# Another order of the first loads, dummy matmuls, and a last row-pass step of 128 queries in an attention and mixture-of-experts kernel

## The chip, the core and the metric

The kernel runs on one core of a Trainium2 chip. The core has a matrix engine (PE, or TensorE), a vector engine (DVE), a scalar engine (ACT) and a general engine (POOL). The profile books the weight loads of PE apart, as PEld. Transfers between the memory of the chip and the core are issued by queues, most of them by the SP queue, and run on 16 DMA engines. The metric is the device time of one execution in microseconds, as the median of several executions.

## What is computed

Three layers follow one another, all in 32-bit floats. The reference, cut to what matters:

```python
# attention: 4 batches, 8 heads, 576 positions, head size 64, causal by blocks of 64
scores = scale * np.matmul(q, k.transpose(0, 1, 3, 2))
scores = np.where(block_i >= block_j, scores, -1000000000.0)
attn = np.exp(scores - np.max(scores, axis=-1, keepdims=True))
attn = attn / (np.sum(attn, axis=-1, keepdims=True) + 1e-09)
x = np.matmul(attn, v)                       # -> rows of 512, 2304 of them
# first mixture: 8 experts (512 -> 1024 -> 512), the two best of noisy logits
logits = x @ w_gate
noisy_logits = logits + np.log1p(np.exp(x @ w_noise)) * noise
out[mask] += top2_w[mask, k, None] * (np.maximum(x[mask] @ w1[e], 0.0) @ w2[e])
# second mixture: 8 experts, the best one, with a bias for each modality
logits = x @ w_gate + modality_bias[modality_id]
out[mask] = gate_w[mask, None] * (np.maximum(x[mask] @ w1[e], 0.0) @ w2[e])
```

## The kernel before

The attention takes the first 280 us or so, the two mixtures the rest. In the attention two heads are worked on together, as a **pair**: 4 batches with 4 pairs each are 16 pairs, numbered p from 0. To keep the accuracy of 32 bits, most operands are split into a high part, rounded to the type fp32r, and a low part, the rest; a product is then three matmuls (high by high, high by low, low by high).

The function `pair` (from line 877) holds the steps of a pair, each with a short name:

- **TQ, TK, T4** on PE transpose the queries, the keys, and the last 64 positions of both (the tiles qld, kld and tld). **QH, KH, A4** on ACT copy the high parts out, **QL, KL, D4** on DVE compute the low parts. The queries go to tiles that the trace calls kp, the keys to kh and kl.
- **S0 to S8** on PE compute the scores of blocks of queries (tile ps; S0 and S2 hold two blocks each, S8 takes two banks). **M** on DVE finds the row maximum (nm), **E** on ACT computes the exponentials (p) and their sums.
- **B0 to B5 and BT** on PE transpose the exponentials, **H** on ACT and **L** on DVE split them (PTh, PTl).
- **VX, V0, V1** on PE multiply by the values (tile pa), **CX, C0, C1** on ACT copy the result out (oT).
- **X0, X1** on PE are the **row pass** (function `xr`, line 1074), one for each head: they turn the 576 columns of oT back into rows and multiply by the gate weights at once, with IW (80 columns) as the moving operand. The stationary operand is a piece of oT: four pieces of 128 queries, and a last one of the 64 queries that remain. **XC0, XC1** on ACT copy the rows out (xu). Each of these matmuls of plain 32-bit floats stands as two instructions in the trace, so that one row pass is ten.

Three PSUM banks serve the scores, three the transposes and the row pass, one the values. A step that needs a bank waits until the one that last used it has been read.

The order of PE, ACT and DVE is written out by a **planner** while the program is built. It keeps a clock for each engine (`clk`), charges each instruction a cost (`pe_cost`, `act_cost`, `dve_cost`, from line 74), and of the steps whose inputs are done takes the one that can start first; among those that can start within 0.15 us it takes the one that is due first by the table SCHED (line 19). For the first pairs it takes the arrival of the loads from a constant, `arrive` (line 1267) plus 5.5 us for each pair; `earliest` (line 1301) uses it, `emit` (line 1279) writes the step. An engine works in that order alone: if one step waits, all that stand behind it on that engine wait. The queue SP is such a line too, and it issues all loads of queries, keys and values (`load`, line 849).

Ahead of the first step, nine dummy matmuls of 512 columns run on PE (line 1108), and the loads of the pairs 0 to 2 are issued in the order keys and queries of 0, values of 0, keys and queries of 1, values of 1, keys and queries of 2. Each load of queries, keys or values is two transfers of 128 KB, and the last 64 positions come in two transfers of 32 KB.

Of the kernel before, what the change touches and what calls it, by code (L numbers as in the profile page):

```python
# [7 lines left out]
F32 = mybir.dt.float32  # L8
# [22 lines left out]
def moe_kernel(tc, q, k, v, w_gate, w_noise, noise, w1, w2, mod_id, w_gate2, mod_bias, m2w1, m2w2, out):  # L31
# [42 lines left out]
    def cols_of(t):  # L74
        n = 1
        for x in t.shape[1:]:
            n *= x
        return n
# [7 lines left out]
    def pe_cost(name, o, i, kw):  # L86
        n = cols_of(o)
        dt = i.dtype
        if name == "transpose":
            return n * .00084  # L90
        return 2 * max(cols_of(i) * .00084, n * .00084) if dt == F32 else n * .000417 + .0145 * (clk["base"] is None)

    def act_cost(name, o, i, kw):
        tables = (not isinstance(kw.get("bias", 0.0), float)) + (not isinstance(kw.get("scale", 0.0), float)) + ("accum_out" in kw)
# [9 lines left out]
    with ExitStack() as top:  # L104
# [6 lines left out]
        LG = dram.tile([NT + CAP, E + 1], F32, name="LG")  # L111


        nc.scalar.preload_act_table_set("natural_log_exp_and_others")
        jp = cst.tile([128, 128], F32, name="jp")
        nc.gpsimd.iota(jp, pattern=[[1, 128]], base=0, channel_multiplier=-1, allow_small_or_imprecise_dtypes=True)
        ident = cst.tile([128, 128], F32, name="ident")
# [686 lines left out]
        with ExitStack() as ph:  # L804
# [41 lines left out]
            def copy(o, i):  # L846
                act.activation(o, i, AF.Copy)

            def load(p, names):
                b, hp = divmod(p, HP)  # L850
                r = L.setdefault(p, {})
                src = {"q": q, "k": k, "v": v}

                if names == "v":
                    r["v"] = ld.tile([128, 5, 2, D], F32, name="vld", bufs=2)
                    tails = [(r["v"][64 * i:64 * i + 64, 4], "v") for i in range(2)]
                else:
                    r["t"] = ld.tile([128, 2, D], F32, name="tld")
                    tails = [(r["t"][64 * i:64 * i + 64], n) for i, n in enumerate("qk")]
                    for n in names:  # L860
                        r[n] = ld.tile([128, 4, 2, D], F32, name=n + "ld")

                def ends():
                    for t, n in tails:
                        nc.sync.dma_start(t, src[n][b, 2 * hp:2 * hp + 2, 512:576, :].rearrange("h p d -> p h d"))
                if p:
                    ends()
                for n in names:
                    for i in range(2):
                        nc.sync.dma_start(r[n][:, 0:4, i, :],  # L870
                                          src[n][b, 2 * hp + i, 0:512, :].rearrange("(c p) d -> p c d", p=128))
                if not p:
                    ends()

            def pair(p):
# [198 lines left out]
                def xr(h):  # L1074
                    def X_():
                        pt = st["x", h] = ps_t.tile([128, 5, DG], F32, name="pt")
                        for c in range(5):
                            n = 128 if c < 4 else 64
                            ten.matmul(pt[0:n, c], st["oT"][:, h, 128 * c:128 * c + n], IW[:, 2 * hp + h], start=True, stop=True)

                    def C_():
                        pt = st["x", h]
                        copy(xu[:, h, 0:4], pt[:, 0:4])
                        copy(xu[0:64, h, 4], pt[0:64, 4])
                        st["xn"] = st.get("xn", 0) + 1
                        if st["xn"] == 2:
                            out_rows()
                    f["X%d" % h], f["XC%d" % h] = X_, C_
# [14 lines left out]


            nc.vector.memset(ones, 1.0)
            pw = ps_s.tile([128, 4, 128], F32, name="ps")
            for _ in range(9):
                nc.tensor.matmul(pw, ones, bc(ones[:, None, :], [128, 4, 128]), start=True, stop=True)
            load(0, "kq")
            load(0, "v")  # L1110
            load(1, "kq")
            load(1, "v")
            load(2, "kq")
            zeros(0, gps)
# [149 lines left out]
            nbank = {"s": bk[0], "t": bk[1], "a": bk[2]}  # L1264
            held = {"s": [], "t": [], "a": []}
            fin, steps = {}, {}
            arrive = dict(zip(("TK", "TQ", "T4"), (4.2, 5.7, 6.8)))
            todo = {e: [] for e in ("pe", "act", "dve")}
            for p in range(NPAIR):
                for n, o in OFF.items():  # L1270
# [8 lines left out]
            def emit(p, n, t):  # L1279
                if p not in steps:  # L1280
                    steps[p] = pair(p) if p < NPAIR else first_steps()
                clk["base"] = t
                steps[p][n]()
                fin[p, n] = clk[engine(n)]
                if n in E_ and all((p, x) in fin for x in E_):
                    emit(p, "R", t)
                if n in ("V0", "V1", "VX") and all((p, x) in fin for x in ("V0", "V1", "VX")) and p + 2 < NPAIR:
                    emit(p + 2, "VS", t)
                if n == "VS" and p + 2 < NPAIR:
                    load(p + 2, "v")  # L1290
                if n in ("TQ", "TK", "T4") and all((p, x) in fin for x in ("TQ", "TK", "T4")) and p < NPAIR:
                    if p + 3 < NPAIR:
                        load(p + 3, "kq")
                    elif p == NPAIR - 1:
                        fetch_b(3)
# [3 lines left out]
                return r[n] if isinstance(r, dict) else r + n[1:]  # L1299

            def earliest(e, p, n):
                t = clk[e] if p > 2 or n not in arrive else max(clk[e], arrive[n] + 5.5 * p)
                for d, k in before[n]:
                    if p >= k:
                        if (p - k, d) not in fin:
# [387 lines left out]
```

## Time and profile before

| | |
|---|---|
| median of three runs | 1004.54 us (1000.55 to 1005.47) |
| the profiled execution | 1002.42 us, its span 1000.6 us |
| PE busy | 955.4 us, 95% |
| DVE, ACT, POOL busy | 723.9, 518.6, 492.9 us |

The span is the time from the first to the last instruction; 1.8 us of the profiled execution lie around it. PE is the busiest engine by far, but a share of 95% hides stages that differ: the first 25 us, in which PE waits and at times runs at a lower granted clock; the pairs that follow, from 34 to 150 us; a stretch from 150 to 250 us in which DVE also routes rows to experts; and the mixtures. The columns of a window are its bounds, its length, the busy time of each engine with the number of instructions, the granted clock of TensorE (1.00 is 2.4 GHz, 0.50 is 1.2 GHz), the busy share of the DMA engines and GB/s. In the first 5 us the clock column reads 1.00 too, but the pace of the dummies says more there: nine of them take 3.89 us, 0.43 us each, and a matmul of 512 columns takes that long at 1.2 GHz.

### The profile page before, as it was taken

What the parts mean: (1) busy time and instruction counts of PE and PEld (TensorE: products, weight loads), DVE (VectorE), ACT (ScalarE), POOL (GpSimd) and SP (SyncE); (2) the same over time, 40 slices, a digit from 0 to 9 for tenths busy, and PEclk for the clock granted to TensorE, in tenths of its full rate; (3) what the DMA queues carried; (4) which work ended last, traced back from release to release, by engine and by line L of the source; (5) the groups of instructions that cost most, each with busy time, mean ns of one, the idle gap of its engine ahead of it and who ended that gap; (6) DMA issues with size and microseconds to landing.
All of it is one profiled execution on the core that took longest, in us unless ns stands there. A gap on an engine that the chain in (4) does not pass through costs nothing.

```text
span 1000.6 us, 17459 instructions
## 1 busy us (share of the span) xinstructions
PE 955.4 (95%) x6058; PEld 863.6 (86%) x6058; DVE 723.9 (72%) x1761; ACT 518.6 (52%) x1156; POOL 492.9 (49%) x400
## 2 busy tenths in 40 slices
PE   7999998898999999999999999999999989999995
PEld 5988898787888997989899898989979879999994
DVE  5878879999968985568493957759788876455450
ACT  5989887778653253333333343333325445555551
POOL 6133141432221589768594857747476254333321
PEclk8999999999999999999999999999999999999998
DMA  5557743331067556555472745534366867776620
GB/s 126 103 156 229 208 122 82 77 82 50 26 202 254 95 138 187 131 138 115 107 147 75 161 105 127 123 80 64 110 149 178 288 215 241 225 223 216 209 84 13
DMA packets 158257, 141.59 MB, mean 142 GB/s; under 512 B 76233, under 2 KB 124745, under 8 KB 158034
## 3 DMA queue, kind: packets, MB, share of 16 engines
q1 hardware_dynamic: 140098, 107.18, 36.4%
q0 software_dynamic: 18064, 33.23, 16.5%
q8 instruction: 50, 0.82, 0.3%
q14 instruction: 45, 0.37, 0.1%
HBM read 112.54 MB, written 28.36 MB: 141 GB/s over the span
## 4 chain that ended last, share of the span: by engine, by line
PE 72%; DVE 13%; issue 5%; ACT 3%; POOL 3%; DMA 2%; SPq 1%; POOLq 0%; ACTq 0%
PE ph L71 28%; PE py L71 26%; PE pt L71 7%; PE ps L71 5%; PE pa L71 3%; PE px L71 2%; DVE nm L71 2%; DVE PTl L71 2%; DVE wl L71 2%; POOL wl L71 2%; ACT p L71 1%; DVE kp L71 1%; DMA xr<-X,ids 1%; ACT wh L71 1%; POOL LG L71 1%
## 5 line engine op out<-in xcount | busy, mean ns | idle before, releaser
L71 POOL TENSOR_TENSOR wl<-raw,wh 128x1024 fp32r<-128x1024 f32 x80 | 207.8, 2628 | 107.7 <-ACT wh L71 93.5
L71 PE MATMUL ph<-xth,wh 128*128 128x320 f32 (+2 forms) x800 | 240.9, 301 | 2.1 <-DVE kp L71 2.1
L71 PE MATMUL ph<-xth,wl 128*128 128x320 f32 (+2 forms) x800 | 239.7, 300 | 0.0
L71 PE MATMUL ph<-xtl,wh 128*128 128x320 f32 (+2 forms) x800 | 239.7, 300 | 0.0
L71 DVE SCALAR_TENSOR_TENSOR zero<-py,gts,wide 128x512 f32<-128x512 f32 x304 | 227.4, 748 | 8.3
L71 PE MATMUL py<-wh,kp 128*128 128x512 f32 x496 | 166.8, 396 | 0.0
L71 PEld LDWEIGHTS ph<-xth,wh 128*128 128x128 f32 x800 | 151.6, 189 | 3.7 <-DVE kp L71 2.9
L71 ACT ACTIVATE wh<-raw 128x1024 fp32r<-128x1024 f32 x144 | 150.9, 1053 | 2.8 <-DMA raw<-in_moe_w_dram 2.8
L71 PEld LDWEIGHTS ph<-xtl,wh 128*128 128x128 f32 x800 | 151.6, 190 | 0.7
L71 PEld LDWEIGHTS ph<-xth,wl 128*128 128x128 f32 x800 | 151.6, 189 | 0.0
L71 ACT ACTIVATE yr<-py,gts 128x512 f32<-128x512 f32 x60 | 41.4, 690 | 144.9 <-PE py L71 96.8
L71 PEld LDWEIGHTS py<-wh,kp 128*128 128x128 f32 x496 | 93.2, 188 | 18.3
L71 DVE SCALAR_TENSOR_TENSOR hl<-ph,hh 128x320 fp32r<-128x320 f32 (+2 forms) x100 | 46.3, 465 | 79.2 <-ACT hh L71 79.0
L71 PE MATMUL ps<-kh,kp 128*128 128x256 f32 (+5 forms) x320 | 98.4, 349 | 3.5 <-ACT p L71 1.5
L71 DVE TENSOR_TENSOR wl<-raw,wh 128x1024 fp32r<-128x1024 f32 x64 | 79.7, 1253 | 29.6 <-ACT wh L71 29.5
L71 PE MATMUL py<-wl,kp 128*128 128x512 f32 x248 | 96.7, 390 | 0.0
L71 POOL DMA_INDIRECT xr<-X,ids x55 | 58.7, 1066 | 72.9 <-PE px L71 44.2
L71 PE MATMUL py<-wh,hh 128*128 128x512 f32 x232 | 93.9, 405 | 0.0
L71 PE MATMUL py<-wl,hh 128*128 128x512 f32 x232 | 90.5, 390 | 1.7 <-POOL wl L71 1.7
L71 PE MATMUL py<-wh,hl 128*128 128x512 f32 x232 | 90.7, 391 | 0.0
L71 ACT ACTIVATE hh<-ph 128x320 fp32r<-128x320 f32 (+2 forms) x100 | 41.9, 418 | 93.6 <-PE ph L71 90.4
L71 DVE TENSOR_TENSOR xtl<-px,xth 128x512 fp32r<-128x512 f32 x58 | 40.0, 689 | 68.1 <-ACT xth L71 68.0
(249 smaller groups left out, 1822.0 us busy)
## 6 DMA issues: line engine op xcount, KB each, us to landing
raw<-in_moe_w_dram SPq DMA_DIRECT2D x144, 512.0 KB, 4.0
X<-zero SPq DMA_DIRECT2D x13, 512.0 KB, 4.3
kld<-in_k_dram SPq DMA_DIRECT2D x32, 128.0 KB, 2.8
qld<-in_q_dram SPq DMA_DIRECT2D x32, 128.0 KB, 2.9
vld<-in_v_dram SPq DMA_DIRECT2D x32, 128.0 KB, 2.7
X<-x SPq DMA_DIRECT2D x16, 256.0 KB, 2.4
wide<-in_moe_w_dram SPq DMA_DIRECT2D x4, 512.0 KB, 4.7
wide<-WG2T POOLq DMA_DIRECT2D x1, 2048.0 KB, 11.6
```

The costliest lines, as they stand in the source:

```text
L71: return f(*a, **kw)
```

## The change

Four edits. The row pass takes as its last piece the last 128 queries of the 576 instead of the last 64 (the first half of them is computed a second time), and the copy behind it reads partitions 64 to 127. The planner's charge for a 32-bit matmul becomes 2 × max(0.09945, 0.00084 × columns). The queries of pair 0 are issued on ACT's queue ahead of ACT's table load, and on SP the keys and queries of pair 1 come ahead of the values of pair 0; the constants `arrive` are replaced by one for each of the pairs 0 to 2. Dummy matmuls: eight instead of nine at the start, in a bank of another pool, and a few more wherever the planner sees PE without work for over 0.6 us in the first 60 us of its clock.

```diff
-        return 2 * max(cols_of(i) * .00084, n * .00084) if dt == F32 else n * .000417 + .0145 * (clk["base"] is None)
+        return 2 * max(.09945, n * .00084) if dt == F32 else n * .000417 + .0145 * (clk["base"] is None)
...
-        nc.scalar.preload_act_table_set("natural_log_exp_and_others")
...
-            def load(p, names):
+            def load(p, names, eng=nc.sync):
...
-                        nc.sync.dma_start(r[n][:, 0:4, i, :],
+                        eng.dma_start(r[n][:, 0:4, i, :],
...
                         for c in range(5):
-                            n = 128 if c < 4 else 64
-                            ten.matmul(pt[0:n, c], st["oT"][:, h, 128 * c:128 * c + n], IW[:, 2 * hp + h], start=True, stop=True)
+                            c0 = 128 * c if c < 4 else S - 128
+                            ten.matmul(pt[:, c], st["oT"][:, h, c0:c0 + 128], IW[:, 2 * hp + h], start=True, stop=True)
...
-                        copy(xu[0:64, h, 4], pt[0:64, 4])
+                        copy(xu[0:64, h, 4], pt[64:128, 4])
...
-            pw = ps_s.tile([128, 4, 128], F32, name="ps")
-            for _ in range(9):
-                nc.tensor.matmul(pw, ones, bc(ones[:, None, :], [128, 4, 128]), start=True, stop=True)
-            load(0, "kq")
+            pw = ps_r.tile([128, 4, 128], F32, name="pt")
+
+            def spin(n):
+                for _ in range(n):
+                    nc.tensor.matmul(pw, ones, bc(ones[:, None, :], [128, 4, 128]), start=True, stop=True)
+            spin(8)
+            clk["pe"] = 4.2
+            load(0, "q", nc.scalar)
+            nc.scalar.preload_act_table_set("natural_log_exp_and_others")
+            load(0, "k")
+            load(1, "kq")
             load(0, "v")
-            load(1, "kq")
             load(1, "v")
             load(2, "kq")
...
-            arrive = dict(zip(("TK", "TQ", "T4"), (4.2, 5.7, 6.8)))
+            arrive = dict(zip(("TK", "TQ", "T4"), ((4.7, 8.2, 15.2), (4.3, 9.2, 16.7), (5.8, 7.2, 17.8))))
...
                 clk["base"] = t
+                if t < 60 and engine(n) == "pe" and t - clk["pe"] > .6:
+                    spin(int((t - clk["pe"] - .3) / .24))
...
-                t = clk[e] if p > 2 or n not in arrive else max(clk[e], arrive[n] + 5.5 * p)
+                t = clk[e] if p > 2 or n not in arrive else max(clk[e], arrive[n][p])
```

What stands in a row on SP, from its first load on. Before:

```order
L870 DMA kld<-in_k_dram 128x4x64 x2
L870 DMA qld<-in_q_dram 128x4x64 x2
L865 DMA tld<-in_q_dram 64x2x64
L865 DMA tld<-in_k_dram 64x2x64
L870 DMA vld<-in_v_dram 128x4x64 x2
L865 DMA vld<-in_v_dram 64x2x64 x2
L865 DMA tld<-in_q_dram 64x2x64
L865 DMA tld<-in_k_dram 64x2x64
L870 DMA kld<-in_k_dram 128x4x64 x2
```

The same place now (the queries of pair 0 are the first two issues on ACT):

```order
L871 DMA kld<-in_k_dram 128x4x64 x2
L866 DMA tld<-in_q_dram 64x2x64
L866 DMA tld<-in_k_dram 64x2x64
L866 DMA tld<-in_q_dram 64x2x64
L866 DMA tld<-in_k_dram 64x2x64
L871 DMA kld<-in_k_dram 128x4x64 x2
L871 DMA qld<-in_q_dram 128x4x64 x2
L871 DMA vld<-in_v_dram 128x4x64 x2
```

The second kld, the keys of pair 1, has moved from the 13th and 14th transfer of SP to the 7th and 8th.

On PE, around TK of pair 1 (kld) and the first scores S4, S6 and S5 of pair 0 (320, 448 and 384 columns; kp_158 and kp_160 are the high and low queries of pair 0, and S0 is the 256). Before:

```order
L71 MATMUL pt<-ident,tld 128x128
L71 MATMUL ps<-kh,kp_158 128x320
L71 MATMUL ps<-kl,kp_158 128x320
L71 MATMUL ps<-kh,kp_160 128x320
L71 MATMUL ps<-kh,kp_158 128x448
L71 MATMUL ps<-kl,kp_158 128x448
L71 MATMUL ps<-kh,kp_160 128x448
L71 MATMUL ps<-kh,kp_158 128x384
L71 MATMUL ps<-kl,kp_158 128x384
L71 MATMUL ps<-kh,kp_160 128x384
L71 MATMUL pt<-ident,kld 128x128 x4
L71 MATMUL ps<-kh,kp_158 128x256
```

Now (kp_157 and kp_159 are those of pair 0):

```order
L71 MATMUL pt<-ident,kld 128x128 x4
L71 MATMUL ps<-kh,kp_157 128x320
L71 MATMUL ps<-kl,kp_157 128x320
L71 MATMUL ps<-kh,kp_159 128x320
L71 MATMUL ps<-kh,kp_157 128x448
L71 MATMUL ps<-kl,kp_157 128x448
L71 MATMUL ps<-kh,kp_159 128x448
L71 MATMUL ps<-kh,kp_157 128x384
L71 MATMUL ps<-kl,kp_157 128x384
L71 MATMUL ps<-kh,kp_159 128x384
L71 MATMUL pt<-ident,tld 128x128
L71 MATMUL pt<-ident,qld 128x128 x4
```

TK of pair 1 has moved ahead of the first scores (with eight dummies ahead of it), and T4 and TQ of pair 1 ahead of S0.

A row pass on PE, with the end of the step VX ahead of it and the start of a score step behind. Before:

```order
L71 MATMUL pa<-PTl,vs 128x256
L71 MATMUL pt<-IW,oT 128x80 x4
L71 MATMUL pt<-IW,oT 64x80
L71 MATMUL ps<-kh,kp_158 128x256
L71 MATMUL ps<-kl,kp_158 128x256
L71 MATMUL ps<-kh,kp_160 128x256
```

Now:

```order
L71 MATMUL pa<-PTl,vs 128x256
L71 MATMUL pt<-IW,oT 128x80 x5
L71 MATMUL ps<-kh,kp_158 128x256
L71 MATMUL ps<-kl,kp_158 128x256
L71 MATMUL ps<-kh,kp_160 128x256
```

The piece of 64 has become a fifth one of 128; nothing else stands there.

## Rows read from the trace of the kernel before

**Rows 1.** The page: span, and PE's busy time, share and instructions.

```profile
span 1000.6 us, 17459 instructions
PE 955.4 (95%) x6058; PEld 863.6 (86%) x6058; DVE 723.9 (72%) x1761; ACT 518.6 (52%) x1156; POOL 492.9 (49%) x400
```

**Rows 2.** Chain of waits, first 30 us: start, duration, what.

```profile
0.73 0.45 SPq L870
...
8.10 0.59 SPq L870
...
8.74 2.65 DMA kld<-in_k_dram
...
12.61 2.51 PE ps L71 x12
```

**Rows 3.** Windows; columns in the first line.

```profile
core 0: us, PE busy (x) PEld busy (x) DVE busy (x) ACT busy (x) POOL busy (x), PEclk, DMA share, GB/s
2.00:4.00 2.00, 2.00 (x6) 0.64 (x5) 0.69 (x1) 0.01 (x1) 1.85 (x6) 1.00 0.87 198
...
11.80:14.50 2.70, 2.70 (x14) 2.70 (x13) 0.42 (x2) 0.65 (x2) 2.46 (x18) 0.50 0.56 128
...
21.90:25.10 3.20, 3.20 (x14) 2.96 (x13) 2.08 (x4) 1.90 (x5) 0.00 (x0) 0.50 0.52 86
...
34.00:150.00 116.00, 111.58 (x820) 102.94 (x818) 90.66 (x222) 101.90 (x314) 36.40 (x53) 1.00 0.61 166
150.00:250.00 100.00, 89.00 (x638) 79.87 (x636) 94.50 (x262) 75.83 (x241) 28.21 (x36) 0.98 0.29 72
```

**Rows 4.** Timeline of PE: start, duration, work, in brackets the idle time ahead.

```profile
1.05 3.89 PE L1108 MATMUL ps<-ones 128*128 128x512 bf16 x9 [1.05 <-DVE ones L1105]
...
5.28 0.63 PE L71 MATMUL pt<-ident,qld 128*128 128x128 f32 x4
...
20.64 0.44 PE L71 MATMUL pt<-ident,p 128*128 128x128 f32 x2 [2.24 <-ACT p L71]
...
36.08 0.66 PE L71 MATMUL pt<-ident,p 128*128 128x128 f32 x4 [0.53 <-DVE PTl L71]
...
40.19 1.29 PE L71 MATMUL pt<-IW,oT 128*128 128x80 f32 x10
```

**Rows 5.** Timeline of ACT and DVE, 7 to 19 us.

```profile
7.17 1.88 DVE L71 SCALAR_TENSOR_TENSOR kp<-pt,kp 64x512 fp32r<-64x512 f32 x4 [0.43 <-ACT kp L71]
...
9.21 1.62 DVE L71 TENSOR_REDUCE nm<-ps 128x1 f32<-128x320 f32 x3
...
9.72 0.53 ACT L71 ACTIVATE p<-ps,nm 128x320 f32<-128x320 f32 x1 [1.87 <-DVE nm L71]
...
12.65 0.60 ACT L71 ACTIVATE kh<-pt 128x512 fp32r<-128x512 f32 x1 [0.96 <-PE pt L71]
14.45 0.31 ACT L71 ACTIVATE p<-ps,nm 128x64 f32<-128x64 f32 x1 [1.20 <-DVE nm L71]
...
15.71 0.45 ACT L71 ACTIVATE kp<-pt 64x64 fp32r<-64x64 f32 x2 [0.50 <-PE pt L71]
...
18.35 0.69 ACT L71 ACTIVATE p<-ps,nm 128x512 f32<-128x512 f32 x1
```

**Rows 6.** Timeline of PE, single instructions at the end of the row pass of Rows 4.

```profile
40.93 0.28 PE L71 MATMUL pt<-IW,oT 128*128 128x80 f32 x1
41.13 0.28 PE L71 MATMUL pt<-IW,oT 128*64 128x80 f32 x1
41.25 0.23 PE L71 MATMUL pt<-IW,oT 128*64 128x80 f32 x1
41.41 0.38 PE L71 MATMUL ps<-kh,kp 128*128 128x256 f32 x1
```

**Rows 7.** Chain of waits by line, 34 to 150 us, then 150 to 280 us.

```profile
by line: PE pt L71 32.4%; PE ps L71 20.9%; PE pa L71 17.8%; DVE PTl L71 5.6%; DVE nm L71 5.2%; ACT p L71 3.7%; issue 2.8%; ACT PTh L71 2.6%; ACT wh L71 2.5%; DVE wl L71 1.7%; DVE kl L71 1.7%; ACT xu L71 0.8%; DVE rr L71 0.7%; ACT oT L71 0.6
...
by line: PE pt L71 18.4%; DVE nm L71 12.7%; PE ps L71 11.1%; DVE PTl L71 10.4%; PE pa L71 9.0%; DVE kp L71 5.2%; DVE sl_ov L71 4.5%; DVE lg L71 2.8%; issue 2.5%; DVE sl_ob L71 2.1%; DVE sl_a L71 2.1%; DVE rr L71 2.0%; DVE ln L71 1.8%; DVE s
```

More of the change, by code (lines that the diff above doesn't have):

```diff
@@ L857, in load @@
                 else:
-                    r["t"] = ld.tile([128, 2, D], F32, name="tld")
-                    tails = [(r["t"][64 * i:64 * i + 64], n) for i, n in enumerate("qk")]
+                    tails = []
+                    if "k" in names:
+                        r["t"] = ld.tile([128, 2, D], F32, name="tld")
+                        tails = [(r["t"][64 * i:64 * i + 64], n) for i, n in enumerate("qk")]
                     for n in names:
@@ L864, in ends @@
                     for t, n in tails:
-                        nc.sync.dma_start(t, src[n][b, 2 * hp:2 * hp + 2, 512:576, :].rearrange("h p d -> p h d"))
+                        eng.dma_start(t, src[n][b, 2 * hp:2 * hp + 2, 512:576, :].rearrange("h p d -> p h d"))
                 if p:
```

## The prediction

> **What bounds the kernel now.** I read the page first: PE is busy for 95% of the span [rows 1], so what shortens PE's work, or its waits, shortens the kernel, if PE is what the stage at hand waits for. Then the windows: from 34 to 150 us PE is busy for 111.6 of 116 us, while DVE has 90.7 and ACT 101.9; from 150 to 250 us DVE is the fullest with 94.5 of 100, and PE has 89.0 [rows 3]. The chain of waits says the same: of its time from 34 to 150 us PE holds 32.4 + 20.9 + 17.8 = 71%, from 150 to 280 us 18.4 + 11.1 + 9.0 = 38.5% [rows 7].
>
> In the first 25 us it is otherwise. The chain there is the SP queue, transfer after transfer from 0.73 us; the first transfer of pair 1's keys is issued at 8.10 us as the 13th, the second at 8.74, and it lands 2.65 us later, at 11.39 [rows 2]. PE waits for it, with S0 and S2 of pair 0 behind it, and when it goes on its clock is granted at 0.50 from 11.8 to 14.5 us; it sits idle once more for 2.24 us ahead of 20.64 us, for exponentials that ACT finished late [rows 4], and then has 0.50 again from 21.9 to 25.1 us [rows 3]. So there are two places to look at: this start, and PE's work in the pairs.
>
> **The charge.** By itself it is nothing. A row pass was charged 4 × 2 × 128 × 0.00084 + 2 × 80 × 0.00084 = 0.994 us and is now charged 5 × 2 × 0.09945 = 0.9945. The orders bear this out: after the first seven pairs PE's steps stand in the same order as before, and in the pairs 1 to 6 only single steps change places. So what the start wins or loses is carried as a shift through everything behind it.
>
> **The row pass.** It is ten instructions, starting at 40.19 us [rows 4]. The first eight, of 128 queries, start 0.11 us apart: (40.93 − 40.19) / 7. From the last of them to the first of 64 it is 0.20 us, to the second 0.12, and to the next step 0.16 [rows 6]: 0.48 us where three more of 128 would take 3 × 0.11 = 0.33. The piece of 64 is the dearer one; the array seems to pay for going from 128 columns to 64 and back. With 128 columns in the last piece each row pass is 0.15 us shorter, and 32 of them give 4.8 us of PE time. Only what lies on the path counts. The upper bound is all of it, 4.8. The lower takes PE's share of the chain: 16 passes × 0.15 × 0.71 + 16 × 0.15 × 0.385 = 2.6. I take **3.0**, nearer to the lower bound, since DVE has the chain in the routing stretch. The copy from partitions 64 to 127 has the shape of the old one, and ACT has slack from 34 us on (101.9 of 116): nothing.
>
> **The start.** Now the keys of pair 1 are the seventh transfer of SP. At (8.10 − 0.73) / 12 = 0.61 us for one issue they start at 4.4 and 5.0 us and land at 5.0 + 2.65 = 7.7 [rows 2], 3.7 us earlier. The head of pair 0 doesn't move with that: its scores S4 wait for its low parts, which DVE had done at about 8.5 us, and the first maximum starts at 9.21 [rows 5]. Now the queries come first (QH ahead of KH, KL behind QL and D4), and the four low parts with the keys' still end at 8.4 to 8.6 by the same durations. TK of pair 1 and eight dummies fill PE's wait up to there. So E4 starts at 9.7 us as it did. What falls away is behind it: of the 8.6 us from E4 to E7 (9.72 to 18.35) ACT sat idle for 0.96 + 1.20 + 0.50 = 2.66 us, and the 0.60 of KH of pair 1 now lie ahead of E4 [rows 5]. With 0.3 us of new waits for maxima E7 starts at 18.35 − 2.66 − 0.60 + 0.3 = 15.4. S8's second half and B0 follow E2 on PE, 0.45 us each, so B0 ends at about 16.4.
>
> From there PE has the same steps to do as before from 20.64 us up to the first row pass at 40.19. These took 19.55 us, of which 0.53 were a wait [rows 4] and half of the 3.2 us at the lower clock [rows 3], 1.6, were lost: 17.4 us of work. With no wait at all the row pass would start at 16.4 + 17.4 = 33.8, **6.4 us earlier**: the upper bound. The lower one is ACT's lead. The split H0 has to wait for B0 now, so that E8 ends at about 18.2 instead of 20.6; if all that follows keeps that distance, low clock included, the lead is **2.4 us**. PE will wait some of it, a few tenths at a time, for exponentials and splits with three banks; but the long idle time that came ahead of the lower clock at 21.9 us is gone, and six dummies stand in the wait ahead of S8. I take the middle, **4.4 us**.
>
> The values of pair 0 land some 2.5 us later, by four more transfers ahead of them; they are first needed at VX, which comes after E8, and have 4 us to spare. The later pairs' loads come in the same order. ACT's table load starts after two issues, some 1 us later, and ACT's first step comes at 5 us: hidden. POOL's queue is not lengthened.
>
> What do two queues give? From 2 to 4 us the DMA engines were busy at 0.87 and moved 198 GB/s [rows 3], and the 512 KB of keys and queries of pair 0 take 2.6 us at that rate whichever queue issues them; the queries, with TQ at 5.28 us [rows 4], can come only some 0.5 us earlier. I count nothing for it, beyond the two issues that SP no longer has ahead of pair 1's keys. The Trainium skill says so too (DMA: Bandwidth & Descriptors, section Issuing engines are not separate DMA queues): transfers from different engines share the same 16 DMA engines, and only issue time is saved. By that rule the sum is mine; were the queues independent, the queries would land beside the keys and the start would win about 0.9 us more, 8.3 in all.
>
> **The sum.** 4.4 + 3.0 = **7.4 us**. The profiled execution of 1002.42 us, with a span of 1000.6, becomes 995.0; it lies 2.1 us below the median of 1004.54, and from the median 1004.54 − 7.4 = **997.1**. With the bounds together it is 2.4 + 2.6 = 5.0 to 6.4 + 4.8 = 11.2 us, 993.3 to 999.5.
>
> **The rivals.**
>
> *Dummies in the way* (0.10). Nothing tells the planner the clock: it charges a dummy 0.24 us, and at the lower clock one takes 3.89 / 9 = 0.43 [rows 4]. Were the clock still low at 6 us, the eight dummies would take 3.4 instead of 1.9, hold TK of pair 1 and S4 up to 9.3 us and cost 1.5; if the lower clock then comes as before, 1.6 more. The start gives 4.4 − 3.1 = 1.3, the sum 4.3: 1000.2. Against it: the queries' four transposes behind the nine dummies of before took 0.63 us [rows 4], the pace of the later ones.
>
> *The 64 was not the price* (0.06). If the 0.48 us at the end of a row pass come from closing its group and not from the width, that edit gives nothing: 4.4, 1000.1. For it there is only one place of that kind; against it, the step of 0.20 stands inside the pass.
>
> *Shift lost later* (0.08). Where DVE holds the chain from 150 to 280 us [rows 7], work that is released early by PE may just wait in its line, and the shift shrinks: half of 7.4, 1000.8. Against it: DVE's work there begins with the pairs, and shifts with them.
>
> *Both at the top* (0.08): 11.2 us, 993.3.
>
> *Slower: a starved PE in the new order* (0.04). In the first pairs BT, which waits for E8, now stands behind the first scores of the next pair. If that order leaves PE waiting for ACT once in each pair as it did ahead of 20.64 us, each wait costs 2.24 us and half of 3.2 us at the lower clock, 3.8 in all. Two waits eat the gain; with four, 15.4 − 7.4 = 8.0 us are lost: 1012.5. Against it: from 34 us on, where the old order is nearly the same, one such wait was 0.53 us [rows 4].
>
> **How the numbers follow.** About 0.5%, 5 us, is what a measurement of this kernel can tell from no change. My forecast has 0.64, within its bounds over 5 us faster; with the top case that makes 0.72 for faster. The three cases of about 4 us, 0.24 together, are no change. The last, 0.04, is slower. The predicted time is that of the forecast, 997.1. For 8 in 10 the range takes in the bounds, about 1 us below them for the runs' spread, and the three cases of 1000 to 1001 us: 992.0 to 1001.5.
>
> **What would show it.** Right: pair 1's keys land at 7.5 to 8.3 us; the first maximum still starts near 9.2; E7 starts near 15.4 and the first row pass between 34 and 37 us; no window up to 34 us at 0.50 after the first 5 us; in a row pass ten starts 0.11 us apart, and the next step 0.11 us behind; PE's busy time from the first row pass to 280 us smaller by nearly 4.8 us. Wrong: dummies 0.43 us apart at 6 to 8 us; a row pass that still takes 1.2 us; a lead at 40 us that is gone at 280 us; idle PE of 2 us ahead of BT in the first pairs.

## The result, and the profile after

The changed kernel takes **992.93 us** as the median (991.95 to 997.72) against 1004.54 (1000.55 to 1005.47): the ratio of the runs is 0.9903, with a 95% interval of 0.9874 to 0.9932. The two medians lie 11.6 us apart, with five runs on either side; the ratio, by which all sizes below go, gives 9.7 us, 7 to 13 with the interval. The forecast was 7.4. The profiled execution takes 992.06 us with a span of 990.3, 10.3 less than the span of [rows 1].

The page of the kernel after, the lines that answer to [rows 1]:

```profile
span 990.3 us, 17496 instructions
PE 949.9 (96%) x6072; PEld 859.5 (87%) x6072; DVE 722.3 (73%) x1761; ACT 521.8 (53%) x1156; POOL 492.1 (50%) x400
```

PE is busy for 5.5 us less, and the span is 10.3 shorter. So about half of the gain is busy time that went (a part of it at the lower clock, and in spite of 14 more dummies), and half is waits that went.

The windows of [rows 3], of the kernel after (bounds, length, PE, PEld, DVE, ACT, POOL busy, granted clock, DMA share, GB/s):

```profile
2.00:4.00 2.00, 2.00 (x6) 0.63 (x5) 0.68 (x1) 1.14 (x1) 1.85 (x6) 1.00 1.10 244
...
11.80:14.50 2.70, 2.46 (x20) 2.22 (x19) 2.10 (x8) 2.58 (x12) 2.50 (x7) 1.00 0.59 134
...
21.90:25.10 3.20, 3.02 (x27) 2.78 (x25) 3.17 (x9) 3.03 (x10) 0.00 (x0) 1.00 0.40 28
...
34.00:150.00 116.00, 112.34 (x833) 104.11 (x831) 93.98 (x236) 106.08 (x325) 33.66 (x49) 1.00 0.65 176
```

The two stretches at 0.50 are at 1.00 now. From 34 to 150 us every engine but POOL is fuller than before: more is done in the same time, with PE idle for 3.7 us instead of 4.4.

How far the kernel after is ahead is read best from the starts of the 32 row passes, which stand in the same order in every kernel here. From the timelines of PE, in us; the lead is the start in the kernel before less the start in the other:

| row pass | before | after | lead |
|---|---|---|---|
| 1st | 40.19 | 36.90 | 3.3 |
| 5th | 70.76 | 67.74 | 3.0 |
| 8th | 93.68 | 87.83 | 5.9 |
| 15th | 140.53 | 133.74 | 6.8 |
| 32nd | 278.36 | 268.55 | 9.8 |
| span | 1000.6 | 990.3 | 10.3 |

So a third of the gain is there at the first row pass, more comes in bit by bit up to 278 us, and the mixtures carry it on. Some of it is the clock: the profile of before has a stretch at 0.50 from 162 to 165 us, over which the lead grows from 7.0 us at the 16th row pass to 8.3 at the 17th. A start that is carried as a shift, and row passes of 0.15 us, don't make this table: 14 of them can give 2.1 us at most, and the lead grew by 3.5 up to the 15th.

### The profile page after: what moved, and what is told of

It reads as the page before. It is cut to its first block, busy times and chain, and to the rows that moved or that the text cites. A ratio compares the mean times of both kernels' runs of the same rounds, so it can differ in the third digit from the quotient of the medians.

```text
span 990.3 us, 17496 instructions
## 1 busy us (share of the span) xinstructions
PE 949.9 (96%) x6072; PEld 859.5 (87%) x6072; DVE 722.3 (73%) x1761; ACT 521.8 (53%) x1156; POOL 492.1 (50%) x400
## 4 chain that ended last, share of the span: by engine, by line
PE 71%; DVE 16%; issue 4%; ACT 4%; POOL 3%; DMA 2%; POOLq 0%; SPq 0%; ACTq 0%
PE ph L71 29%; PE py L71 27%; PE pt L71 5%; PE ps L71 4%; DVE nm L71 3%; DVE PTl L71 3%; PE pa L71 2%; PE px L71 2%; DVE wl L71 2%; DVE kp L71 2%; POOL wl L71 2%; ACT p L71 1%; DMA xr<-X,ids 1%; ACT wh L71 1%; DVE sl_ob L71 1%
## 5 line engine op out<-in xcount | busy, mean ns | idle before, releaser
L71 PE MATMUL ps<-kh,kp 128*128 128x256 f32 (+5 forms) x320 | 95.6, 340 | 1.5 <-ACT p L71 1.2
```

The costliest lines, as they stand in the source:

```text
L71: return f(*a, **kw)
```

## The experiments

All ratios are against the kernel before, timed beside it on the same chip (three groups of runs, with medians of 1002.95, 1002.16 and 1002.44 us). A ratio is turned into time with 1003 us. All kernels compute everything. The number in brackets behind a ratio is its 95% interval.

### The row pass alone

On the kernel before, with the charge and the copy that belong to it; every other instruction stays in its place:

```diff
-        return 2 * max(cols_of(i) * .00084, n * .00084) if dt == F32 else ...
+        return 2 * max(.09945, n * .00084) if dt == F32 else ...
...
-                            n = 128 if c < 4 else 64
-                            ten.matmul(pt[0:n, c], st["oT"][:, h, 128 * c:128 * c + n], IW[:, 2 * hp + h], start=True, stop=True)
+                            c0 = 128 * c if c < 4 else S - 128
+                            ten.matmul(pt[:, c], st["oT"][:, h, c0:c0 + 128], IW[:, 2 * hp + h], start=True, stop=True)
...
-                        copy(xu[0:64, h, 4], pt[0:64, 4])
+                        copy(xu[0:64, h, 4], pt[64:128, 4])
```

> The kernel before with the row pass of 128 queries last and the new charge, and nothing of the start; every engine's order is that of before. Theory: going to 64 columns and back costs 0.19 us a pass (1.22 against 1.03 us from a pass's start to the next step), and nearly all of the 32 passes lie on the path, so the lead over before is 0 at the first row pass, about 6 us at the last, and the time about 998.5 us. Rival: only the passes on PE's share of the chain count, 0.71 of those up to 150 us and 0.385 behind: 16 x 0.19 x 0.71 + 16 x 0.19 x 0.385 = 3.3 us, 1001.2.

Measured: 999.44 us, 0.9969 (0.9954 to 0.9984): 3.1 us faster. The size of one pass is seen in the timelines of PE. Before, the 5th row pass and the step behind it (start, duration, work):

```profile
70.76 1.29 PE L71 MATMUL pt<-IW,oT 128*128 128x80 f32 x10
71.99 0.38 PE L71 MATMUL ps<-kh,kp 128*128 128x256 f32 x1
```

The same two in the kernel after:

```profile
67.74 1.24 PE L71 MATMUL pt<-IW,oT 128*128 128x80 f32 x10
68.77 0.36 PE L71 MATMUL ps<-kh,kp 128*128 128x256 f32 x1
```

From start to start it is 1.23 us before and 1.03 now: 0.20 us less, not 0.15; 32 of them are 6.4 us. About half of it counted, 3.1 us. PE's waits from 38 to 145 us (line waited for: us in all, times, longest), in the kernel before:

```profile
PE pt L71 <- DVE kl L71: 2.4, 3, 0.9
PE pt L71 <- ACT wide L71: 0.7, 1, 0.7
PE pt L71 <- ACT xu L71: 0.5, 1, 0.5
PE pt L71 <- ACT p L71: 0.4, 1, 0.4
```

and with the row pass alone:

```profile
PE pt L71 <- DVE kl L71: 3.2, 3, 1.2
PE pt L71 <- ACT xu L71: 0.8, 1, 0.8
PE pt L71 <- ACT wide L71: 0.7, 1, 0.7
PE pt L71 <- ACT p L71: 0.4, 1, 0.4
```

The same four waits have grown from 4.0 to 5.1 us. What PE wins, DVE and ACT don't, and PE waits for their low parts and copies the longer. That is part of the answer: from the first to the 15th row pass the lead grows by 0.8 us where 14 passes save 2.8, and 1.1 of the missing 2.0 are these waits. The rest, and what becomes of the passes behind 145 us, was not traced.

### The start alone

The kernel after with the old row pass; its orders are those of the kernel after:

```diff
-                            c0 = 128 * c if c < 4 else S - 128
-                            ten.matmul(pt[:, c], st["oT"][:, h, c0:c0 + 128], IW[:, 2 * hp + h], start=True, stop=True)
+                            n = 128 if c < 4 else 64
+                            ten.matmul(pt[0:n, c], st["oT"][:, h, 128 * c:128 * c + n], IW[:, 2 * hp + h], start=True, stop=True)
...
-                        copy(xu[0:64, h, 4], pt[64:128, 4])
+                        copy(xu[0:64, h, 4], pt[0:64, 4])
```

> The changed kernel with the old row pass of 64 queries last; every engine's order is that of the changed kernel. Theory: the start's lead of 3.3 us at the first row pass is carried unchanged to the end, 1004.5 - 3.3 = 1001.2; up to 1.5 us more if the stretch at the lower clock that the trace of before shows at 162 to 165 us stays away. Rival: the lead grows along the pairs because an earlier start gives the later stages slack, 6 to 8 us at the last row pass, 997 to 998.5.

Measured: 995.56 us, 0.9933 (0.9915 to 0.9951): 6.7 us faster, so that the two parts add up to the whole (3.1 + 6.7 = 9.8 of 9.7). But this is not a shift: the lead is 4.0 us at the first row pass, 3.5 at the fifth and 6.9 at the 15th, where no work was taken from PE. Its waits from 38 to 145 us say where the 3 us came from; one is left:

```profile
PE pt L71 <- ACT wide L71: 0.7, 1, 0.7
```

The four waits of before, 4.0 us, have become 0.7: 3.3 us. Something in this half of the change takes away waits between 70 and 130 us, far behind the start. The orders differ there: the next two runs go for it. In the kernel after as a whole the waits between 38 and 145 us are 1.9 us:

```profile
PE pt L71 <- DVE kl L71: 1.0, 3, 0.4
PE pt L71 <- ACT wide L71: 0.7, 1, 0.7
PE pt L71 <- DVE PTh L71: 0.2, 1, 0.2
```

### The old arrival constants

The kernel after, with the arrivals told to the planner as before (5.5 us for each pair). But for the dummies the order of PE is then that of the kernel before, from PE's first step on; the new loads, dummies and row passes stay:

```diff
-            arrive = dict(zip(("TK", "TQ", "T4"), ((4.7, 8.2, 15.2), (4.3, 9.2, 16.7), (5.8, 7.2, 17.8))))
+            arrive = dict(zip(("TK", "TQ", "T4"), ((4.2, 9.7, 15.2), (5.7, 11.2, 16.7), (6.8, 12.3, 17.8))))
```

> The changed kernel with the old arrival constants: new loads, dummies and row pass, but from the first row pass on PE's steps stand in the order of before. Theory: the new constants' order of the pairs 3 to 5 is what removes PE's waits for DVE's kl between 60 and 110 us; here they stay, the lead over before is 3 to 5 us at the first row pass and grows by no more than 1 us up to 145 us, as in the run with the row pass alone: 997 to 998. Rival: an earlier start alone does it, and the lead grows as in the changed kernel: 993.

Measured: 995.84 us, 0.9934 (0.9912 to 0.9956), 3.1 us less of a gain than the whole change has (3.0 less than the kernel with one queue below, which was timed beside it and has the later order of the change; either difference has an interval of 3 us or more to both sides, so that the traces and the next run have to bear it out). Its lead is 3.9 at the first row pass and 4.7 at the 15th, and its waits from 38 to 145 us are to the digit those of the row pass alone (3.2, 0.8, 0.7 and 0.4). So the order gave the rest. How much of the lead at the first row pass is the new start and how much is the clock is told further down.

### The order alone

The other way round: the kernel before, with old loads and old row pass, where only the due times of the constants and of the weights' transfers and splits are 1 us later in the planner's clock. PE's order up to the first row pass is that of before, behind it that of the kernel after:

```diff
-            for t, f in ((14, consts1), (34, consts2), (50, consts3)):
+            for t, f in ((14, consts1), (35, consts2), (51, consts3)):
...
-                at(50 + 14 * i, lambda: stage.fetch(1))
-                at(50 + 14 * i + 11, lambda: stage.split(vec))
+                at(51 + 14 * i, lambda: stage.fetch(1))
+                at(62 + 14 * i, lambda: stage.split(vec))
```

> The kernel before, with the old start and the old row pass; only the planner's due times of the constants and of the first weights' loads and splits are 1 us later (35, 51, 51 + 14 i, 62 + 14 i). PE's steps up to the first row pass stand as before, and behind it in the order of the changed kernel. Theory: that order is worth 3 us by itself: the lead over before is 0 at the first row pass and about 3 at the 15th, PE's waits for DVE's kl between 60 and 110 us go, and the time is 3 us under that of before, 999. Rival: the order only pays together with the early start; here it gives nothing or loses, 1002 to 1003.

Measured: 999.10 us, 0.9974 (0.9959 to 0.9989): 2.6 us, by a table of due times alone. The lead grows from 3.1 at the 5th row pass to 5.0 at the 15th, by 1.9; the waits have fallen from 4.0 to 2.1 us, by 1.9 too:

```profile
PE pt L71 <- DVE kl L71: 1.4, 2, 0.9
PE pt L71 <- ACT wide L71: 0.7, 1, 0.7
```

How the two orders differ is seen ahead of the 6th row pass. PE before:

```profile
72.80 0.60 PE L71 MATMUL pt<-ident,kld 128*128 128x128 f32 x4
73.15 0.48 PE L71 MATMUL ps<-kh,kp 128*128 128x512 f32 x1
...
76.95 1.40 PE L71 MATMUL pt<-IW,oT 128*128 128x80 f32 x10 [0.85 <-DVE kl L71]
```

and PE in the kernel after:

```profile
69.57 0.60 PE L71 MATMUL pt<-ident,kld 128*128 128x128 f32 x4
...
73.28 1.34 PE L71 MATMUL pt<-IW,oT 128*128 128x80 f32 x10 [0.30 <-DVE kl L71]
74.42 0.48 PE L71 MATMUL ps<-kh,kp 128*128 128x512 f32 x1
```

The 512 scores have moved behind the row pass. The row pass needs the bank that the keys' transposes (kld) filled and that DVE empties with kl. DVE before, from its weight split (wl) to kl:

```profile
72.70 1.29 DVE L71 TENSOR_TENSOR wl<-wide,wh 128x512 fp32r<-128x512 f32 x2 [1.66 <-ACT wh L71]
73.91 0.69 DVE L71 TENSOR_TENSOR PTl<-pt,PTh 128x512 fp32r<-128x512 f32 x1
...
76.21 0.69 DVE L71 TENSOR_TENSOR kl<-pt,kh 128x512 fp32r<-128x512 f32 x1
```

and DVE in the kernel after:

```profile
68.17 0.69 DVE L71 TENSOR_TENSOR PTl<-pt,PTh 128x512 fp32r<-128x512 f32 x1 [0.16 <-ACT PTh L71]
...
69.95 1.29 DVE L71 TENSOR_TENSOR wl<-wide,wh 128x512 fp32r<-128x512 f32 x2 [0.76 <-ACT wh L71]
...
72.54 0.69 DVE L71 TENSOR_TENSOR kl<-pt,kh 128x512 fp32r<-128x512 f32 x1
```

In both the row pass starts 0.74 us behind the start of kl. But kl starts 3.41 us behind the transposes before (76.21 − 72.80), and 2.97 after (72.54 − 69.57): the low part PTl now lies ahead of the weight split, not between it and kl. With the order alone this one wait stayed (0.86 us, at 73.97), while those for xu and p (0.46 at 90.82, 0.40 at 82.95 in the kernel before) and the two others for kl (0.86 at 108.48, 0.65 at 123.92) went, and a new one of 0.59 came at 89.31. So the order is shown to be the cause, but the swap above is not what the run with the order alone lives on; which swap takes away which wait was not taken apart.

### Keys first, alone

The kernel before with pair 1's keys and queries ahead of pair 0's values, and nothing else:

```diff
             load(0, "kq")
+            load(1, "kq")
             load(0, "v")
-            load(1, "kq")
```

> The kernel before with one thing changed: on SP the keys and queries of pair 1 come ahead of the values of pair 0. PE, DVE and ACT have the order of before. Theory: the earlier keys give the wait of 1.3 us ahead of 11.53 us back and perhaps one of the stretches at the lower clock, some 1.5 to 3 us at the first row pass; as the order of the pairs 3 to 5 is still the old one, PE's waits of 2.4 us for DVE's kl between 60 and 110 us stay and the lead does not grow: 1000 to 1001.5. Rival: the earlier phase alone removes those waits, and the lead grows by 3 us, 997 to 998.

Measured: 1000.81 us, 0.9986 (0.9971 to 1.0001): 1.4 us, with an interval that just takes in no gain at all. In its profile the lead is 3.0 us at the first row pass and stays there, to 0.1, up to the 15th, with the four waits of before unchanged: that is what a shift looks like. That its profile shows more than its runs can be put down to the clock: from 5 to 40 us the profile of before was granted 0.90 in the mean, this one 0.95.

### Without the dummies in the waits

The kernel after without the 15 dummies that stand in PE's waits; the eight at the very start stay:

```diff
-                if t < 60 and engine(n) == "pe" and t - clk["pe"] > .6:
-                    spin(int((t - clk["pe"] - .3) / .24))
```

> The changed kernel with the eight dummies at the start but without the 15 that the planner puts into PE's later waits. Theory: with PE idle in those waits the granted clock falls to 0.50 once in the first 30 us, as it did in the kernel before, for about 3 us, and the kernel is 1.3 to 1.6 us slower than the changed one. Rival: the work between the waits is enough, the clock stays at 1.00 and the time is that of the changed kernel; or the dummies stood in the way of the transposes of pair 1's keys, and it is a little faster.

Measured: 993.33 us, 0.9910 (0.9895 to 0.9926), the same as with them. In its profile the clock fell, as the windows show:

```profile
5.00:8.00 3.00, 1.17 (x9) 0.97 (x9) 0.68 (x1) 1.88 (x4) 2.45 (x8) 0.91 0.68 155
8.00:14.00 6.00, 5.20 (x19) 4.73 (x20) 4.23 (x9) 2.33 (x9) 2.84 (x7) 0.50 0.60 134
```

PE was idle for most of 5 to 8 us and had 0.50 behind it (from 5 to 40 us it was granted 0.90 in the mean, the kernel after 1.00); the first row pass started 1.1 us later than in the kernel after (37.98 against 36.90). The timed runs show no such difference: it may be too small for them, or the drop does not come in each. The dummies in the waits are not shown to pay.

### One queue

The kernel after with the queries of pair 0 on SP, ahead of the keys:

```diff
-            load(0, "q", nc.scalar)
+            load(0, "q")
```

> The changed kernel with all loads on SP, the queries of pair 0 first and then its keys; the orders of PE, DVE and ACT are the same. Theory: two queues give only issue time and make keys and queries land together at 5.2 us; on one queue the queries land at about 4, the keys at about 5.2, TQ starts a microsecond earlier, and all later transfers start 1.1 us later: the first maximum comes within 0.5 us of 10.9, the time within 1 us of the changed kernel. Rival: the second queue is worth its 1.1 us of issue time on the path: 1 us slower.

Measured: 992.12 us, 0.9904 (0.9883 to 0.9925): the same. PE and DVE in its timeline:

```profile
4.43 1.06 PE L71 MATMUL pt<-ident,qld 128*128 128x128 f32 x4
9.09 0.63 PE L71 MATMUL pt<-ident,kld 128*128 128x128 f32 x4 [1.04 <-DMA kld<-in_k_dram]
10.20 0.49 DVE L71 TENSOR_REDUCE nm<-ps 128x1 f32<-128x320 f32 x1 [0.73 <-PE ps L71]
35.76 1.34 PE L71 MATMUL pt<-IW,oT 128*128 128x80 f32 x10 [0.65 <-DVE PTl L71]
```

The queries are transposed 0.8 us earlier than over two queues, where they share the way with the keys, and pair 1's keys a little later. Two more kernels told the planner of the loads on one queue. With queries first:

```diff
-            load(0, "q", nc.scalar)
+            load(0, "q")
...
-            arrive = dict(zip(("TK", "TQ", "T4"), ((4.7, 8.2, 15.2), (4.3, 9.2, 16.7), (5.8, 7.2, 17.8))))
+            arrive = dict(zip(("TK", "TQ", "T4"), ((5.3, 8.2, 15.2), (4.2, 9.2, 16.7), (6.2, 7.2, 17.8))))
```

> All loads on SP as in the run before the last, and the constants for pair 0 set to what that gives (queries 4.2, keys 5.3, last positions 6.2), which changes the order up to the second row pass. Theory: the order of the later pairs is that of the changed kernel, so its time follows from the lead at the first row pass: between 2 us slower and 1.5 us faster than the changed kernel. It is a try at a faster version as much as a test of how far the first order can move the end.

Measured: 995.39 us, 0.9932 (0.9910 to 0.9955), 2.8 us less of a gain than one queue with the constants of the change, which are further from the truth. The interval of that difference is 3 us, so it is hardly clear of noise. Its waits for kl from 38 to 145 us are 2.7 us, where the kernel after has 1.0. And with keys first:

```diff
-            load(0, "q", nc.scalar)
...
-            load(0, "k")
+            load(0, "kq")
...
-            arrive = dict(zip(("TK", "TQ", "T4"), ((4.7, 8.2, 15.2), (4.3, 9.2, 16.7), (5.8, 7.2, 17.8))))
+            arrive = dict(zip(("TK", "TQ", "T4"), ((4.4, 8.2, 15.2), (5.3, 9.2, 16.7), (6.0, 7.2, 17.8))))
```

> The changed kernel with all loads on SP, pair 0's keys first and then its queries, as in the kernel before, and the constants of pair 0 set to that (keys 4.4, queries 5.3); PE's order is that of the changed kernel but for TK ahead of TQ and one dummy less. Theory: the keys' high and low parts are done while the queries still load, as in the kernel before, so the first maximum comes about 1 us earlier than 10.9 and the time is 0.5 to 1.5 us under the changed kernel. Rival: the first maximum still waits for the dummies and the transposes of pair 1's keys that stand ahead of it, and nothing is won.

Measured: 994.28 us, 0.9918 (0.9890 to 0.9946). That is 1.4 us less of a gain than one queue with queries first, well inside the noise. The first maximum comes hardly earlier than in the kernel after (10.77 against 10.92), since the scores stand behind pair 1's keys there too, and these come later:

```profile
9.65 0.63 PE L71 MATMUL pt<-ident,kld 128*128 128x128 f32 x4 [1.91 <-DMA kld<-in_k_dram]
10.77 0.49 DVE L71 TENSOR_REDUCE nm<-ps 128x1 f32<-128x320 f32 x1 [1.34 <-PE ps L71]
```

### Another narrow piece

BT also has a piece of 64 columns. The kernel after, without it, and the copy behind it taken from partitions 64 to 127 twice:

```diff
                     ten.transpose(st["bt"], P[8][:, 448:576], ident)
-                    ten.transpose(st["bt"][0:64], P[8][:, 512:576], ident)
...
-                f.update(BT=BT, HT=lambda: act.activation(end, st["bt"], AF.Copy),
+                f.update(BT=BT, HT=lambda: [act.activation(end[d], st["bt"][64:128], AF.Copy) for d in (slice(0, 64), slice(64, 128))],
```

> The changed kernel, and the step BT without its second transpose, the only one left on PE with 64 columns: ACT copies the high part out of partitions 64 to 127 twice instead. PE saves one transpose and the way to 64 columns and back in each of 16 pairs, ACT pays one more copy of 64 x 128, about 0.28 us a pair. Theory that width on PE is the price and PE is the path: about 0.2 us a pair, 3 us faster than the changed kernel. Rival: ACT, busy for 106 of 116 us in the pairs, becomes the path, and it is the same or up to 4 us slower.

Measured: 996.73 us, 0.9943 (0.9927 to 0.9959): 4 us slower than the kernel after. What is saved on PE seems to be paid on ACT; its splits PTh from 36 to 280 us are (busy us, mean ns, then idle us ahead) after:

```profile
L71 ACT ACTIVATE PTh<-pt 128x512 fp32r<-128x512 f32 (+1 forms) x113 | 53.3, 508 | 15.7 <-PE pt L71 15.0
```

and in this kernel:

```profile
L71 ACT ACTIVATE PTh<-pt 128x384 fp32r<-128x384 f32 (+2 forms) x128 | 58.1, 483 | 10.5 <-PE pt L71 9.0
```

4.8 us more on ACT, which was busy for 106 of 116 us from 34 us on, and another order besides, which was not taken apart from it. So the price on ACT is argued, not shown.

## Why the prediction came out as it did

The time lies in the range, near its lower end, and the sign was right. By parts:

| part | predicted | measured | by |
|---|---|---|---|
| row pass | 3.0 | 3.1 (± 1.5) | row pass alone |
| loads, dummies, head | 4.4 | 3.5 (± 2.7), most of it the clock | old arrivals less row pass alone, 6.6 − 3.1 |
| order of the pairs behind | 0 | 2.6 (± 1.5), 3.1 (± 3.6) | order alone; whole less old arrivals |
| sum | 7.4 | 9.2 to 9.7 | 9.7 for the whole |

**Two steps failed.** The first is the one under the charge: "in the pairs 1 to 6 only single steps change places. So what the start wins or loses is carried as a shift". The order was read, and its change was costed at nothing, without a bound on either side, although the waits that hang on it, 4.0 us between 38 and 145, could be read in the trace of before. The runs showed 2.6 to 3.1 us in its place. The planner writes pairs against due times that stand still; the new arrival constants shift its clock, and steps fall on the other side of a weight split: due times that are 1 us later give PE the very order that the kernel after has from the first row pass on. It is a gain of chance, since nothing in the change aims at it. That the time lies near the lower end of the range is in part owed to this term, which the forecast did not have.

**The row pass.** The piece of 64 was the price, as [rows 6] had it, and the rival that it was not falls. One pass saves 0.20 us instead of 0.15. A part of that is the step behind it, which was to follow the last piece by 0.11 us: in the first pass of the kernel after it starts at 38.04, 0.07 behind the last piece at 37.97, against 0.16 in [rows 6]. Half of the 6.4 us lies on the path: the term of 3.0 came out right by luck, by two errors that offset each other, a price too low and a share too high (3.0 of 4.8 is 62%; 3.1 of 6.4 is 48%).

**The head** is the second step that failed. The first maximum was to stay near 9.2 us [rows 5]; it came 1.7 later, as ACT, DVE and PE show in the timeline of the kernel after:

```profile
5.20 1.09 PE L71 MATMUL pt<-ident,qld 128*128 128x128 f32 x4 [0.55 <-DMA qld<-in_q_dram]
6.32 1.20 ACT L71 ACTIVATE kp<-pt 64x512 fp32r<-64x512 f32 x2 [3.18 <-PE pt L71]
7.54 0.60 ACT L71 ACTIVATE kh<-pt 128x512 fp32r<-128x512 f32 x1
7.55 1.88 DVE L71 SCALAR_TENSOR_TENSOR kp<-pt,kp 64x512 fp32r<-64x512 f32 x4 [4.87 <-ACT kp L71]
9.04 0.63 PE L71 MATMUL pt<-ident,kld 128*128 128x128 f32 x4
9.44 0.82 DVE L71 TENSOR_TENSOR kl<-pt,kh 128x64 fp32r<-128x64 f32 x2
10.92 0.49 DVE L71 TENSOR_REDUCE nm<-ps 128x1 f32<-128x320 f32 x1 [0.65 <-PE ps L71]
16.75 0.69 ACT L71 ACTIVATE p<-ps,nm 128x512 f32<-128x512 f32 x1
...
36.90 1.34 PE L71 MATMUL pt<-IW,oT 128*128 128x80 f32 x10 [0.65 <-DVE PTl L71]
```

PE waits for the queries up to 5.20, while before it had the keys' transposes at 4.78; the queries' transposes then take 1.09 us instead of 0.63 [rows 4], their matmuls 0.22 us apart, which is the lower pace, up to about 6.5 us; ACT then does the queries ahead of the keys, and the keys' low parts on DVE come last, at 9.44 to 10.3. Only 0.5 us earlier or later was thought of, for the landing; that the keys would stand on PE behind queries that come no earlier, and at the lower pace, was not. What was said of the steps behind holds: E7 came 1.35 late, at 16.75 instead of 15.4, less than the head; and the first row pass, at 36.90, lies in the 34 to 37 us that were named.

**The start against the clock.** The lead of 3.3 us at the first row pass is not what the forecast meant by it. The run with the order alone has the old start, and in its profile the clock does not fall: E7 starts at 16.83 there and the first row pass at 37.05, against 16.75 and 36.90 in the kernel after. Where the clock does not fall on either side, the new start is worth 0.15 us by these two, and 0.8 us with the profiles of the start alone (36.23) and of the old arrival constants (36.30). The timed runs agree. Each has its mean granted clock on record. Over the 53 runs of the kernel before it lies between 0.987 and 0.997, and a run that has 0.001 more is shorter by some 0.75 us. The mean over the runs is 0.992 for the kernel before, 0.991 with the row pass alone, 0.995 with the old arrival constants, and 0.993 with the order alone. By that rate the clock makes up an estimated 2.7 of the 3.5 us of the start, 2 of the 9.7 of the whole, over 1 of the 1.4 of keys first alone, and under 0.5 of the 2.6 of the order alone. So the term of 4.4 came near by luck: the earlier keys, from which it was worked out, gave less than 1 us by these numbers, and a clock that falls less often the rest. Which part of the new start keeps the clock up was not taken apart.

**The checks.** Pair 1's keys landed at 8.0 us (the second transfer is issued at 5.15 and takes 2.9 us), within the 7.5 to 8.3 that were named. The clock column has no 0.50 up to 34 us, but the pace of the transposes says that the lower clock lasted to 6.5 us. PE's busy time between the first and the last row pass fell from 220.99 to 215.16 us, 5.8, where 4.8 was named. The price per pass (31 × 0.20 = 6.2) and the stretch at the lower clock at 162 us in the profile of before would make it more than that; what offsets them was not traced.

**The rivals.** Dummies in the way: not in the profile of the kernel after, where the eight start 0.22 us apart (all in 1.89 us). But it happened in the profile of "Another narrow piece", whose PE has the same order up to there, as its timeline shows:

```profile
7.65 3.07 PE L1110 MATMUL pt<-ones 128*128 128x512 bf16 x8
```

The first six of these start 0.43 us apart, and TK of pair 1 starts at 10.55 instead of 9.04, the 1.5 us of that rival. The nine dummies of before had brought the pace up by 5 us; whether a ninth would have done so here was not tested. Shift lost later: no, the lead is kept through the mixtures. Starved PE: no, the wait of 2.2 us ahead of BT is gone rather than repeated. Both at the top gave 993.3 and so hit the time, but not by its mechanism: neither term reached its top; a third was missing.

**Two queues** are worth nothing that can be measured, as the sum had it. The Trainium skill (DMA: Bandwidth & Descriptors, section Issuing engines are not separate DMA queues) says that transfers from different engines interleave on the same 16 DMA engines; the run with one queue agrees, with 0.9904 against 0.9903.

## What to carry to other kernels

Where a program's order is written by a planner with fixed due times, any constant that shifts its clock is an edit to the whole order: read the waits that stand in the moved stretch and put a bound on them, to both sides, even if "only single steps change places". A kernel whose busiest engine is at 95% still gives back only a part of what that engine saves; look which waits grow, and count the saving against them. When a change wins more than its parts explain, try the parts' side effects alone: here moving a few due times by 1 us gave 2.6 us with none of the change in it. And before a lead in a profile is put down to an earlier load, compare it with a profile of the old start at the same granted clock.

## What the hardware showed that was not expected

**The lower clock comes and goes.** The kernel with only the later due times has the same instructions on PE in the same order as the kernel before up to the first row pass. It has the wait of 2.23 us for ACT as well, at 19.11 us, but no fall of the clock behind it:

```profile
19.11 0.44 PE L71 MATMUL pt<-ident,p 128*128 128x128 f32 x2 [2.23 <-ACT p L71]
...
37.05 1.30 PE L71 MATMUL pt<-IW,oT 128*128 128x80 f32 x10
```

Its windows have the granted clock in the third column from the right:

```profile
12.00:14.00 2.00, 2.00 (x21) 2.00 (x19) 0.78 (x4) 1.11 (x4) 1.88 (x13) 1.00 0.59 133
...
22.00:24.00 2.00, 2.00 (x19) 1.96 (x18) 2.00 (x5) 1.72 (x6) 0.00 (x0) 1.00 0.48 106
```

These stretches were at 0.50 in the profile of before [rows 3], and its first row pass came at 40.19 [rows 4]: 3.1 us between two executions of the same start. By the clock column the mean from 5 to 40 us was 1.00 in all seven profiles with the loads and all the dummies of the change or with these loads on one queue; it was 0.90 in the one without the dummies in the waits, and with the old start 0.90 twice (before, row pass alone) and 1.00 once; keys first alone lies between, with 0.95. So the dummies seem to keep the clock up, but what decides it stays open. A lead in one profile is good to 3 us only. The sizes above go by the timed runs, and these too hold a share of clock.

**A piece of 64 columns** between pieces of 128 costs 0.20 us in a pass of ten instructions, 1.23 us against 1.03 with twice the columns in the last piece. The Trainium skill (TensorEngine Tiling (Array Packing), section Tiling Modes, Key Properties) says that a change of tiling mode drains TensorE. The steps of 0.20 and 0.16 us on either side of the narrow piece [rows 6], where 0.11 is usual, agree with it; it gives no price.

**Two queues move more and deliver no earlier.** From 2 to 4 us they moved 244 GB/s against 198 before [rows 3], but the queries alone on one queue, ahead of the keys, were transposed at 4.43 us, and beside the keys at 5.20.
